# A sliding-window attention block on one core: weighted values started ahead of the second softmax, with a fixed order on a shared port

## The chip, the core and the metric

The kernel runs on one core of a Trainium2 chip. The engines are called by the names of the profile: PE (TensorE, matmuls), DVE (VectorE), ACT (ScalarE), POOL (GpSimd) and SP (the queue that issues most DMAs). In this program SBUF is the memory that the engines work from, and PSUM, of eight banks, the one that matmuls write to. The metric is device microseconds of one execution. Each of the kernels in the experiments ran beside the kernel before on the same chip.

## The reference, cut to what matters

```python
xn = layernorm(x)                       # x: 1 x 2048 x 640
q, k, v = split(xn @ wqkv)              # 32 heads of 20
# each position sees 8 positions: its own, 2 back, 4 back, ... 14 back
logits = einsum("bhsd,bhswd->bhsw", q, k[window]) * scale
attn = softmax(logits, axis=-1)
o = einsum("bhsw,bhswd->bhsd", attn, v[window])
A = o @ wo
B = ((xn @ w_gate) * (xn @ w_up)) @ w_down      # 640 -> 1536 -> 640
return x + A + B
```

The large matmuls (projections, gate and up, down) are TensorE's. The window part is elementwise: products of q with shifted k on VectorE, their head sums as small matmuls, softmax on VectorE and ScalarE, then attention times shifted v on VectorE, the sum of two window halves on GpSimd, and again a head sum as small matmuls.

## The kernel before

The kernel does not write its instructions in order. Small generators yield tasks with priorities and dependencies; a scheduler with a model of durations (`occ`, in us) picks the order for each engine once, when the program is built, and puts in the semaphore waits. On the chip each engine then runs its fixed list. In the program, `lock` marks the instructions that are to be kept apart: VectorE steps with both inputs in SBUF, and GpSimd's; the changed kernel calls what they share a port. These are the parts that the change and the argument touch:

```python
def calm():            # may GpSimd read SBUF now? not during a softmax
    return all(("sm", x) in done or count.get(("logits", x), 0) < 2 for x in range(2))

def tokens():          # every add waits for the end of the softmaxes already placed
    return [("tok", x) for x in range(2) if ("sm", x) in done]

# softmax step on VectorE, both inputs in SBUF, lock=True: not beside a GpSimd op in the model
op("dve", lambda e: e.tensor_tensor(o, a, b, f), r=[a, b], w=[o], name=name, occ=occ, lock=True)

BATCH = (1, 4, 9, 14, 19)               # units after which head sums are made
def unit(u):                            # 20 units: 4 row blocks x 5 chunks of channels
    ...
    def mul(x, r0, nr):                 # attention (in PSUM) times shifted values (in SBUF)
        op("dve", lambda e: e.tensor_tensor(p, vw, a, ALU.mult), ..., occ=0.09 + 1.1 * nr)
    def add(x):                         # sum of the two window halves
        op("pool", lambda e: e.tensor_tensor(o, p[:, :, 0, :], p[:, :, 1, :], ALU.add), ..., occ=2.36, lock=True)
    ...
def sums(us):                           # head sums: 4 matmuls with 128x32 weights for each unit
    ...
    yield Task("pe", go, ..., banks=len(us), slack=0.7)
```

The head sums use one quarter of TensorE's columns at a time, so each batch of them sits in another tiling mode than the large matmuls around it. Of the eight PSUM banks two hold the attention weights; a batch of five units wants five of the other six at once.

Of the kernel before, what the change touches and what calls it, by code (L numbers as in the profile page):

```python
# [49 lines left out]
class Sched:  # L50
# [5 lines left out]
    def __init__(self, nc):  # L56
# [7 lines left out]
        self.t_lock = 0.0  # L64
        self.t_data = 0.0
# [42 lines left out]
    def deps_of(self, eng, rk, wk):  # L108
# [6 lines left out]
        for k in wk:  # L115
            st = self.state.get(k)
            if st is None:
                continue
            o, rds = st
            if o is not None and not (eng == "pe" and o.eng == "pe"):  # L120
                deps[o.idx] = o
            for q in rds:
                if inorder and q.eng == eng and not q.dma and eng != "dve":
                    continue
                deps[q.idx] = q
        return deps

    def op(self, eng, fn, r=(), w=(), dma=False, name="", occ=None, lat=None, lock=False, nbytes=0, mode=0, group=None, extra=0.0, acc=0.0, land=None):
# [7 lines left out]
        deps = self.deps_of(eng, rk, wk)  # L136
        if occ is None and not dma:
            occ = 0.1
# [45 lines left out]
        if dma:  # L184
# [7 lines left out]
            else:  # L192
                g = self.groups[group]
                g[1].append(X)
                X.event = (g[0], 16)
        self.ops.append(X)
# [152 lines left out]
def build_kernel(nc, A_x, A_wqkv, A_wo, B_x, B_w_gate, B_w_up, B_w_down, out):  # L349
# [43 lines left out]
    sv_free = list(range(NS))  # L393
# [69 lines left out]
    def dma(o, i, r=(), w=(), name="", eng="sp", group=None, land=None):  # L463
# [10 lines left out]
       r=[IDENT[:]], w=[IDENT[:]], name="ident", occ=0.4)  # L474
    op("pool", lambda e: e.memset(G[:], 0.0), w=[G[:]], name="g0", occ=0.2)
# [58 lines left out]
    def front(t):  # L534
# [11 lines left out]

        def sqrt():
            op("act", lambda e: e.activation(sd, mv[:, 1:2], ACT.Sqrt, bias=EPSC[:, 0:1]), r=[("mv", t), EPSC[:]],  # L548
               w=[("sd", t)], name=f"sd{t}", occ=0.25)
            mark("sd", t)  # L550

        def recip():
            op("dve", lambda e: e.reciprocal(rstd, sd), r=[("sd", t)], w=[("rstd", t)], name=f"rstd{t}", occ=0.16)
            mark("rstd", t)
            if t >= N_DVE_A:
                op("dve", lambda e: e.tensor_scalar(nmr, mv[:, 0:1], rstd, -1.0, op0=ALU.mult, op1=ALU.mult),
                   r=[("mv", t), ("rstd", t)], w=[("nmr", t)], name=f"nmr{t}", occ=0.13)
# [27 lines left out]
        yield Task("act", sqrt, r=[("mv", t)], prio=p - 1)  # L585
        yield Task("dve", recip, r=[("sd", t)], prio=p)
# [192 lines left out]
    def calm():  # L779
        return all(("sm", x) in done or count.get(("logits", x), 0) < 2 for x in range(2))  # L780

    def tokens():
        return [("tok", x) for x in range(2) if ("sm", x) in done]
# [7 lines left out]
    def products():  # L791
        rows = {j: [] for j in range(NJ)}
        holds = {}
        for j, kind in ORDER:
# [4 lines left out]
            else:  # L799
                if len(QUAD.get(j, ())) == 2 and j not in holds:  # L800
# [4 lines left out]
            if len(rows[j]) == 10 - 3 * len(QUAD.get(j, ())):  # L805
                K.spawn(logits(j, rows[j]))

# [17 lines left out]
    def q_bank(j, c, hold):  # L825
# [7 lines left out]
        def copy():  # L833
            evac([(QT[:, j, c, :], PS[:, hold[0], :], JB)], f"qev{j}_{c}")
# [13 lines left out]
    def wide(j, slots, hold):  # L848
        halves = [(r, q0) for r in QUAD[j] for q0 in (0, 2)]
        acc, parts = {}, {1: [], 0: []}  # L850
        for c0 in (0, 2):
            for i, (r, q0) in enumerate(halves):
                f = []
                for c in (c0, c0 + 1):
                    yield lambda: len(hold[c]) > 0 and len(usable(j)) > 0
                    k = slot(j)
# [6 lines left out]
                    def go(o=o, qb=qb, kv=kv, q=q, rk=rk):  # L863
                        X = op("dve", lambda e: e.tensor_tensor(o[:], qb, kv, ALU.mult), r=[q, rk], w=[o[:]],  # L864
# [50 lines left out]
    def logits(j, slots):  # L915
# [7 lines left out]
        def go(*bs):  # L923
            for i, e in enumerate(slots):
                n, s, r = e[:3]
                b, i, nt = bs[1 - r], i - (0 if r else n1), n1 if r else len(slots) - n1
                for a in range(4):
                    o = PS[32 * a:32 * a + 32, b, :].rearrange("p (q s) -> p q s", q=4)
                    x = s[:, :, a * TS:(a + 1) * TS]
                    op("pe", (lambda o, x, i, a: lambda e: e.matmul(o, G[:], x, start=(i == 0), stop=(i == nt - 1),  # L930
                                                                   tile_position=(0, 32 * a)))(o, x, i, a),
# [25 lines left out]
    def softmax(x):  # L957
        def tt(o, a, b, f, name, occ):
            return Task("dve", lambda: op("dve", lambda e: e.tensor_tensor(o, a, b, f), r=[a, b], w=[o], name=name, occ=occ,
                                          lock=True), r=[a, b], w=[o], prio=10, lock=True)  # L960
# [8 lines left out]
        def sub():  # L969
            op("dve", lambda e: e.tensor_tensor(L[:], L[:], bc(M3[:], 8), ALU.subtract), r=[L[:], m3], w=[L[:]], name="lsub",  # L970
               occ=1.2, lock=True)

        def exp():
            op("act", lambda e: e.activation(L[:], L[:], ACT.Exp), r=[L[:]], w=[L[:]], name="exp", occ=1.9)

        def recip():
            op("act", lambda e: e.activation(s3, s3, ACT.Ln), r=[s3], w=[s3], name="rln", occ=0.4)
            op("act", lambda e: e.activation(R, s3, ACT.Exp, scale=-1.0), r=[s3], w=[R], name="rs", occ=0.4)
# [431 lines left out]
```

## Time and profile before

The time before is 268.65 us (median of runs, 268.47 to 268.7).

| | before |
|---|---|
| span of the profiled run | 266.8 us |
| PE busy | 261.3 us (98%) |
| DVE, POOL, ACT busy | 82%, 50%, 40% |
| POOL's adds: first starts, last ends | 131.05, 244.42 us |
| last head sums start | 244.42 us in the chain |

To read it: 98% on TensorE and a list of its waits in which no other engine stands after the first 10 us say that every microsecond of matmul is a microsecond of the kernel. The other engines matter only when they are late. By the starts in the trace, the last unit's four head sums begin at 245.22 us, 0.8 us after its last add ends, so there was next to no slack.

### The profile page before, as it was taken

How to read it: one execution, taken by the hardware profiler on the slowest of the kernel's cores; microseconds unless marked ns; L12 is line 12 of the kernel's file. 1: busy time of each engine (PE TensorE's matmuls, PEld its weight loads, DVE VectorE, ACT ScalarE, POOL GpSimd, SP SyncE). 2: the span in 40 equal slices, each digit the busy share in tenths (PEclk: the TensorE clock that was granted, in tenths of full speed). 3: DMA queues.
4: the chain of work that ended last, by engine and by line, in shares of the span. 5: the costliest groups of instructions: out<-in, count | busy, mean ns of one | idle time of the engine just before them, and what ended most of it. 6: DMA issues, size and time to landing. Idle time of an engine off the chain costs nothing.

```text
span 266.8 us, 4468 instructions
## 1 busy us (share of the span) xinstructions
PE 261.3 (98%) x1771; PEld 152.6 (57%) x1788; DVE 218.3 (82%) x278; ACT 107.6 (40%) x193; POOL 132.4 (50%) x83
## 2 busy tenths in 40 slices
PE   7999999999999999999999999999999999999996
PEld 5996965444444444444444446764577547754775
DVE  4678899999999996379999899988998999981221
ACT  3469998556732122255434442007500460016000
POOL 1000000000007359700399999977999799979000
PEclk9999999999999999999999999999999999999999
DMA  7974789502226997193426733656345633130101
GB/s 213 374 207 81 195 107 371 213 0 98 101 49 161 192 234 178 9 333 81 114 49 142 170 80 87 185 162 168 80 129 152 184 96 89 49 98 2 49 27 49
DMA packets 40933, 35.75 MB, mean 134 GB/s; under 512 B 16080, under 2 KB 39120, under 8 KB 40912
## 3 DMA queue, kind: packets, MB, share of 16 engines
q1 hardware_dynamic: 40096, 33.31, 46.0%
q0 software_dynamic: 576, 2.10, 4.1%
q8 instruction: 14, 0.23, 0.4%
q10 hardware_dynamic: 240, 0.05, 0.1%
q14 instruction: 7, 0.06, 0.1%
HBM read 25.07 MB, written 5.26 MB: 114 GB/s over the span
## 4 chain that ended last, share of the span: by engine, by line
PE 96%; DVE 1%; DMA 1%; issue 1%; ACT 0%
PE PS L1195 39%; PE PS L1277 28%; PE PS L655 22%; PE PS L930 3%; PE PS L687 2%; PE PS L1144 2%; DMA XST<-in_A_x_dram 1%; PE PS L599 0%; DVE STATS L542 0%; ACT XNT L611 0%; DVE XNS L563 0%; DVE XNT L609 0%; DVE FOUT L1290 0%; ACT SD L548 0%; DVE MV L545 0%
## 5 line engine op out<-in xcount | busy, mean ns | idle before, releaser
L1096 POOL TENSOR_TENSOR SV<-PV 128x1024 bf16<-128x1024 f32 x40 | 93.2, 2361 | 20.4 <-DVE LOG L981 19.4
L1091 DVE TENSOR_TENSOR PV<-VX,PS 128x1024 f32<-128x1024 bf16 (+1 forms) x56 | 91.9, 1669 | 2.5 <-POOL SV L1096 2.3
L655 PE MATMUL PS<-XNT,WQKV 128*128 128x512 bf16 (+2 forms) x384 | 60.2, 315 | 0.4 <-issue 0.2
L1195 PE MATMUL PS<-XNT,WG 128*128 128x512 bf16 x238 | 59.4, 379 | 0.2
L1195 PE MATMUL PS<-XNT,WU 128*128 128x512 bf16 x231 | 57.7, 379 | 0.4 <-issue 0.2
L655 PEld LDWEIGHTS PS<-XNT,WQKV 128*128 128x128 bf16 x390 | 37.9, 112 | 21.8 <-ACT LOG L941 0.8
L1195 PEld LDWEIGHTS PS<-XNT,WG 128*128 128x128 bf16 x240 | 23.3, 98 | 28.5 <-issue 0.8
L1195 PEld LDWEIGHTS PS<-XNT,WU 128*128 128x128 bf16 x240 | 23.4, 98 | 28.2 <-ACT LOG L941 0.4
L819 DVE TENSOR_TENSOR PRD<-QT,KT 128x2048 bf16<-128x2048 bf16 x32 | 36.8, 1215 | 0.0
L1290 DVE TENSOR_TENSOR FOUT<-PS,XR 128x320 bf16<-128x320 f32 (+1 forms) x33 | 15.7, 477 | 18.4 <-PE PS L1277 18.3
L1277 PE MATMUL PS<-WD,HT 128*128 128x320 bf16 x192 | 28.5, 299 | 0.0
L660 ACT ACTIVATE HT<-PS 128x512 bf16<-128x512 f32 x24 | 14.3, 596 | 31.6 <-PE PS L1195 31.6
L1277 PE MATMUL PS<-WO,OT 128*128 128x320 bf16 (+1 forms) x165 | 26.6, 295 | 0.0
L890 POOL TENSOR_TENSOR PRF<-PRF,PRF 128x1024 f32<-128x1024 f32 x4 | 9.4, 2348 | 31.2 <-DVE PRF L864 31.2
L660 ACT ACTIVATE UX<-PS 128x512 bf16<-128x512 f32 x14 | 8.4, 597 | 39.5 <-PE PS L1195 39.5
L949 POOL MEMSET LOG<- 32x6 bf16 (+6 forms) x7 | 0.4, 96 | 47.6 <-ACT LOG L941 47.6
L1204 DVE TENSOR_TENSOR HT<-HT,PS 128x512 bf16<-128x512 bf16 x23 | 15.7, 684 | 9.5 <-PE PS L1195 7.4
L1277 PEld LDWEIGHTS PS<-WD,HT 128*128 128x128 bf16 x192 | 18.6, 98 | 8.0 <-issue 0.4
L1277 PEld LDWEIGHTS PS<-WO,OT 128*128 128x128 bf16 x165 | 15.9, 98 | 5.9
L864 DVE TENSOR_TENSOR PRF<-PS,KT 128x1024 f32<-128x1024 f32 x16 | 19.0, 1216 | 0.3 <-DMA PRF<-PRF 0.3
L660 ACT ACTIVATE XNT<-PS 128x512 bf16<-128x512 f32 x12 | 7.2, 598 | 25.5 <-PE PS L1195 25.5
L542 DVE BATCH_NORM_STATS2 STATS<-XST 128x6 f32<-128x320 bf16 x32 | 14.6, 472 | 2.5 <-DMA XST<-in_A_x_dram 2.5
(62 smaller groups left out, 235.7 us busy)
## 6 DMA issues: line engine op xcount, KB each, us to landing
VX<-v_scratch SPq DMA_DIRECT2D x80, 130.0 KB, 2.9
XST<-in_A_x_dram SPq DMA_DIRECT2D x16, 160.0 KB, 5.7
v_scratch<-VST SPq DMA_DIRECT2D x4, 640.0 KB, 4.2
XR<-in_A_x_dram SPq DMA_DIRECT2D x16, 160.0 KB, 2.7
out_dram<-FOUT SPq DMA_DIRECT2D x15, 160.0 KB, 1.8
PRF<-PRF POOLq DMA_DIRECT2D x4, 512.0 KB, 8.7
WG<-in_B_w_gate_dram SPq DMA_DIRECT2D x1, 1920.0 KB, 8.6
WU<-in_B_w_up_dram SPq DMA_DIRECT2D x1, 1920.0 KB, 12.0
```

Of the source, the lines that this page charges most:

```text
L542: op("dve", lambda e: e.bn_stats(o, a), r=[a], w=[("st", t, i)], name=f"bn{t}_{i}", occ=0.49)
L655: op("pe", (lambda o, l, x, c, first: lambda e: e.matmul(o, l, x, start=first, stop=(c == NCH - 1)))(o, l, x, c, first), r=[l, x], w=[o], ...
L660: X = op("act", (lambda o, i: lambda e: e.activation(o, i, ACT.Copy))(o, i), r=[i], w=[o], name=name, occ=0.12 + n * 0.9e-3)
L819: op("dve", lambda e: e.tensor_tensor(s[:], qb, kv, ALU.mult), r=[q, rk], w=[s[:]], name=f"prod{j}_{r}_{c}", occ=1.15, lock=True)
L864: X = op("dve", lambda e: e.tensor_tensor(o[:], qb, kv, ALU.mult), r=[q, rk], w=[o[:]], name=f"prow{j}_{r}_{c}_{q0}", occ=1.17)
L890: yield Task("pool", lambda: op("pool", lambda e: e.tensor_tensor(x, x, y, ALU.add), r=[x, y] + tokens(), w=[x], name=name, occ=2.36, lock ...
L1091: op("dve", lambda e: e.tensor_tensor(p, vw, a, ALU.mult), r=[vv] + rk, w=[p], name=f"pv{u}_{x}_{r0}", occ=0.09 + 1.1 * nr)
L1096: X = op("pool", lambda e: e.tensor_tensor(o, p[:, :, 0, :], p[:, :, 1, :], ALU.add), r=[p[:]] + tokens(), w=[o], name=f"pva{u}_{x}", occ= ...
L1195: op("pe", (lambda l, x, c: lambda e: e.matmul(PS[:, b, :], l, x, start=(c == 0), stop=(c == NCH - 1)))(l, x, c), r=[l, x], w=[PS[:, b, :] ...
L1204: X = op("dve", lambda e: e.tensor_tensor(h, h, PS[:, hold[1], :], ALU.mult), r=[h, PS[:, hold[1], :]], w=[h], name=f"h{m}_{j}", occ=0.65)
L1277: op("pe", (lambda l, x, i: lambda e: e.matmul(dst, l, x, start=(i == 0), stop=(i == n - 1)))(l, x, i), r=[l, x], w=[PS[:, b, :]], name=f" ...
L1290: X = op("dve", lambda e: e.tensor_tensor(o, PS[:, b, 0:wid], xr, ALU.add), r=[PS[:, b, :], xr], w=[o], name=f"fin{t}_{nb}", occ=0.15 + wi ...
```

## The change

Its intent is to use GpSimd's 19.4 idle us ahead of and during the second softmax. The model's `calm` (no add during a softmax) becomes a rule that fits an add into a gap when it does not push the next softmax step by more than 0.3 us, and explicit waits make VectorE and GpSimd alternate on the chip in just that order. The first adds go to two output buffers that nobody else needs by then. With early adds, the first head sums can be one batch of five. Beside that, square roots and reciprocals of the layer norm are made for pairs of tiles.

```diff
+        if lock:
+            deps.update({d.idx: d for d in self.port["pool" if eng == "dve" else "dve"]})
...
-    sv_free = list(range(NS))
+    sv_free = [3, 4, 0, 1, 2]
...
-    def calm():
-        return all(("sm", x) in done or count.get(("logits", x), 0) < 2 for x in range(2))
+    def room(occ, ready=0.0):
+        def f():
+            if count.get(("logits", 0), 0) >= 2 and ("sm", 0) not in done:
+                return False
+            return due[0] == INF or max(K.t["pool"], K.t_lock, ready) + occ <= due[0] + SLIP
+        return f
+    calm = room(2.36)
     def tokens():
-        return [("tok", x) for x in range(2) if ("sm", x) in done]
+        return []
...
-    BATCH = (1, 4, 9, 14, 19)
+    BATCH = (4, 9, 14, 19)
     def vx_loads():
-        yield num(NJ, "lg")
+        yield have("products")
...
+    GROUPS = ((4, 5), (6, 7), (8, 9), (10, 11), (12, 13), (14, 15))
```

(Cut: the selection matrix made by GpSimd at the start, some ordering of ScalarE's reads, the time of the residual's loads, the place of the first two attention copies, and the rule that lets multiplications of gate and up go to GpSimd earlier.)

More of the change, by code (lines that the diff above doesn't have):

```diff
@@ L64, in __init__ @@
         self.t_lock = 0.0
+        self.port = {"dve": [], "pool": []}
         self.t_data = 0.0
@@ L122, in deps_of @@
             for q in rds:
-                if inorder and q.eng == eng and not q.dma and eng != "dve":
+                if inorder and q.eng == eng and not q.dma and eng != "dve" and not (eng == "act" and k[0] == "ps"):
                     continue
@@ L195, in op @@
                 X.event = (g[0], 16)
+        if lock:
+            self.port[eng] = [X] if eng == "dve" else self.port[eng] + [X]
+            if eng == "dve":
+                self.port["pool"] = []
         self.ops.append(X)
@@ L474, in build_kernel @@
        r=[IDENT[:]], w=[IDENT[:]], name="ident", occ=0.4)
+    op("pool", lambda e: e.memset(SEL[:], 0.0), w=[SEL[:]], name="sel", occ=0.1)
+    for q in range(4):
+        op("pool", (lambda q: lambda e: e.affine_select(SEL[:], SEL[:], pattern=[[-1, 32]], compare_op=ALU.not_equal, fill=1.0,
+                                                        base=-32 * q, channel_multiplier=1))(q),
+           r=[SEL[:]], w=[SEL[:]], name=f"sel{q}", occ=0.2)
     op("pool", lambda e: e.memset(G[:], 0.0), w=[G[:]], name="g0", occ=0.2)
@@ L545, in aggr @@
             op("dve", lambda e: e.bn_aggr(mv, st), r=[("st", t, 0), ("st", t, 1)], w=[("mv", t)], name=f"bnag{t}", occ=0.2)
+        ts = next((g for g in GROUPS if t in g), (t,))
+        t0, t1 = ts[0], ts[-1] + 1
         def sqrt():
-            op("act", lambda e: e.activation(sd, mv[:, 1:2], ACT.Sqrt, bias=EPSC[:, 0:1]), r=[("mv", t), EPSC[:]],
-               w=[("sd", t)], name=f"sd{t}", occ=0.25)
-            mark("sd", t)
+            o, i = SD[:, t0:t1, 0:1], MV[:, t0:t1, 1:2]
+            op("act", lambda e: e.activation(o, i, ACT.Sqrt, bias=EPSC[:, 0:1]), r=[("mv", k) for k in ts] + [EPSC[:]],
+               w=[("sd", k) for k in ts], name=f"sd{t}", occ=0.25)
+            for k in ts:
+                mark("sd", k)
         def recip():
-            op("dve", lambda e: e.reciprocal(rstd, sd), r=[("sd", t)], w=[("rstd", t)], name=f"rstd{t}", occ=0.16)
-            mark("rstd", t)
+            o, i = SD[:, t0:t1, 1:2], SD[:, t0:t1, 0:1]
+            op("dve", lambda e: e.reciprocal(o, i), r=[("sd", k) for k in ts], w=[("rstd", k) for k in ts], name=f"rstd{t}", occ=0.16)
             if t >= N_DVE_A:
-                op("dve", lambda e: e.tensor_scalar(nmr, mv[:, 0:1], rstd, -1.0, op0=ALU.mult, op1=ALU.mult),
-                   r=[("mv", t), ("rstd", t)], w=[("nmr", t)], name=f"nmr{t}", occ=0.13)
+                n, m = SD[:, t0:t1, 2:3], MV[:, t0:t1, 0:1]
+                op("dve", lambda e: e.scalar_tensor_tensor(n, m, -1.0, o, op0=ALU.mult, op1=ALU.mult),
+                   r=[x for k in ts for x in (("mv", k), ("rstd", k))], w=[("nmr", k) for k in ts], name=f"nmr{t}", occ=0.13)
+            for k in ts:
+                mark("rstd", k)
         def apply():
@@ L584, in front @@
         yield Task("dve", aggr, r=[("st", t, 1)], prio=p)
-        yield Task("act", sqrt, r=[("mv", t)], prio=p - 1)
-        yield Task("dve", recip, r=[("sd", t)], prio=p)
+        mark("mv", t)
+        if t == ts[-1]:
+            yield Task("act", sqrt, r=[("mv", t)], prio=p - 1)
+            yield Task("dve", recip, r=[("sd", t)], prio=p)
+        yield have("rstd", t)
         if t >= NXN:
@@ L777, in slot @@
         return n
-    def calm():
-        return all(("sm", x) in done or count.get(("logits", x), 0) < 2 for x in range(2))
+    INF = 1e9
+    due = [INF]
+    def room(occ, ready=0.0):
[5 more added lines that the diff above has]
+    calm = room(2.36)
     def tokens():
-        return [("tok", x) for x in range(2) if ("sm", x) in done]
+        return []
     def k_view(j, r, c, q0, nq):
@@ L793, in products @@
         holds = {}
-        for j, kind in ORDER:
+        for at, (j, kind) in enumerate(ORDER):
             if kind == "w":
@@ L799, in products @@
             else:
-                if len(QUAD.get(j, ())) == 2 and j not in holds:
+                if len(QUAD.get(j, ())) == 2 and j not in holds and (j, "w") == ORDER[at + 1]:
                     yield from fetch(j, 0, holds.setdefault(j, {c: [] for c in range(4)}))
@@ L806, in products @@
                 K.spawn(logits(j, rows[j]))
+        mark("products")
     def narrow(j, r, c, slots):
@@ L833, in copy @@
         def copy():
-            evac([(QT[:, j, c, :], PS[:, hold[0], :], JB)], f"qev{j}_{c}")
+            o, i = QT[:, j, c, :], PS[:, hold[0], :]
+            op("act", lambda e: e.activation(o, i, ACT.Copy), r=[i], w=[o, ("qev", j, c)], name=f"qev{j}_{c}", occ=0.58)
             for _ in range(4):
@@ L855, in wide @@
                     yield lambda: len(hold[c]) > 0 and len(usable(j)) > 0
+                    yield num(4, "qk", 0, j, c)
                     k = slot(j)
@@ L863, in go @@
                     def go(o=o, qb=qb, kv=kv, q=q, rk=rk):
-                        X = op("dve", lambda e: e.tensor_tensor(o[:], qb, kv, ALU.mult), r=[q, rk], w=[o[:]],
+                        X = op("dve", lambda e: e.tensor_tensor(o[:], qb, kv, ALU.mult), r=[q, rk, ("qev", j, c)], w=[o[:]],
                                name=f"prow{j}_{r}_{c}_{q0}", occ=1.17)
@@ L929, in go @@
                     x = s[:, :, a * TS:(a + 1) * TS]
-                    op("pe", (lambda o, x, i, a: lambda e: e.matmul(o, G[:], x, start=(i == 0), stop=(i == nt - 1),
-                                                                   tile_position=(0, 32 * a)))(o, x, i, a),
+                    op("pe", (lambda o, x, i, a, nt: lambda e: e.matmul(o, G[:], x, start=(i == 0), stop=(i == nt - 1),
+                                                                   tile_position=(0, 32 * a)))(o, x, i, a, nt),
                        r=[G[:], x], w=[o], name=f"lg{j}_{r}_{i}_{a}", occ=0.054, lat=0.4, mode=1)
@@ L958, in tt, with go @@
         def tt(o, a, b, f, name, occ):
-            return Task("dve", lambda: op("dve", lambda e: e.tensor_tensor(o, a, b, f), r=[a, b], w=[o], name=name, occ=occ,
-                                          lock=True), r=[a, b], w=[o], prio=10, lock=True)
+            def go():
+                X = op("dve", lambda e: e.tensor_tensor(o, a, b, f), r=[a, b], w=[o], name=name, occ=occ, lock=True)
+                due[0] = INF if name == "ssum3" else X.end
+            return Task("dve", go, r=[a, b], w=[o], prio=10, lock=True)
         L = LOG[x]
@@ L971, in sub @@
                occ=1.2, lock=True)
+            due[0] = INF
         def exp():
-            op("act", lambda e: e.activation(L[:], L[:], ACT.Exp), r=[L[:]], w=[L[:]], name="exp", occ=1.9)
+            X = op("act", lambda e: e.activation(L[:], L[:], ACT.Exp), r=[L[:]], w=[L[:]], name="exp", occ=1.9)
+            due[0] = X.end
         def recip():
             op("act", lambda e: e.activation(s3, s3, ACT.Ln), r=[s3], w=[s3], name="rln", occ=0.4)
-            op("act", lambda e: e.activation(R, s3, ACT.Exp, scale=-1.0), r=[s3], w=[R], name="rs", occ=0.4)
+            X = op("act", lambda e: e.activation(R, s3, ACT.Exp, scale=-1.0), r=[s3], w=[R], name="rs", occ=0.4)
+            due[0] = X.end
         def attn():
-            op("dve", lambda e: e.tensor_tensor(L[:], L[:], bc(RS[:], 8), ALU.mult), r=[L[:], R], w=[L[:], ("tok", x)], name="attn",
+            op("dve", lambda e: e.tensor_tensor(L[:], L[:], bc(RS[:], 8), ALU.mult), r=[L[:], R], w=[L[:]], name="attn",
                occ=1.2, lock=True)
+            due[0] = INF
         def move():
@@ L992, in softmax @@
         yield num(2, "logits", x)
+        if x:
+            due[0] = max([0.0] + [d.end for d in K.deps_of("dve", K.keys(L[:]), ()).values()])
         if x:
@@ L1040, in weighted @@
         yield have("atx", 0)
+        yield have("products")
         def take(a, b):
@@ L1045, in weighted, with at_copy @@
         yield Task("act", take, banks=2, prio=0, contig=True)
+        for r in range(2):
+            yield Task("act", lambda: at_copy(0, r), r=[ATX[0][:, 0, r, :]], w=[PS[:, at_bank[r], :]], prio=1)
         for u in range(NU):
             yield from unit(u)
+    def at_copy(j, r):
+        o, i = PS[:, at_bank[r], :], ATX[j // 2][:, j % 2, r, :]
+        op("act", lambda e: e.activation(o, i, ACT.Copy), r=[i], w=[o], name=f"atp{j}_{r}", occ=0.55)
     def unit(u):
@@ L1056, in unit @@
             sv_free.extend(range(NS, len(SV)))
-        yield lambda: len(sv_free) > 0
+        yield lambda: len(sv_free) > 0 and (sv_free[0] in (3, 4) or count.get(("lg",), 0) >= NJ)
         sv_of[u] = sv_free.pop(0)
@@ L1072, in unit @@
         v = VX[:, u % NVX]
-        def at_copy(r):
-            o, i = PS[:, at_bank[r], :], ATX[j // 2][:, j % 2, r, :]
-            op("act", lambda e: e.activation(o, i, ACT.Copy), r=[i], w=[o], name=f"atp{j}_{r}", occ=0.55)
         def mul(x, r0, nr):
@@ L1108, in adder @@
             yield Task("pool", lambda: add(x), r=[slots[x][:]], w=[sv[:, 2 * x:2 * x + 2, :]], prio=10, lock=True)
-        if c in (0, NCH - 1):
+        if c == NCH - 1 or (c == 0 and j):
             for r in range(2):
                 if c == 0:
-                    yield Task("act", lambda: at_copy(r), r=[ATX[j // 2][:, j % 2, r, :]],
+                    yield Task("act", lambda: at_copy(j, r), r=[ATX[j // 2][:, j % 2, r, :]],
                                w=[PS[:, at_bank[r], :]], prio=1)
@@ L1163, in on_pool @@
     def on_pool(j, m):
-        return ("sm", 1) in done and m < 11 and ucount[0] - count.get(("hp",), 0) < HP_MAX
+        return count.get(("lg",), 0) >= NJ and m < 11 and ucount[0] - count.get(("hp",), 0) < HP_MAX
     def gu(j):
@@ L1220, in pmul @@
                     def pmul():
-                        op("pool", lambda e: e.tensor_tensor(h, h, us, ALU.mult), r=[h, us], w=[h], name=f"hp{m}_{j}",
+                        op("pool", lambda e: e.tensor_tensor(h, h, us, ALU.mult), r=[h, us] + tokens(), w=[h], name=f"hp{m}_{j}",
                            occ=1.15, lock=True)
@@ L1227, in after @@
                     yield num(k0, "hp")
-                    yield calm
+                    yield room(1.15)
                     yield Task("pool", pmul, r=[h, us], w=[h], prio=HP_PRIO, lock=True)
@@ L1238, in xr_loads @@
     def xr_loads():
-        yield have("xnt", NT - 1)
+        yield num(NJ, "lg")
         yield have("vx", NVX)
@@ L1311, in dn_piece @@
         K.spawn(tail())
+    SLIP = 0.3
     N_PE_T = 4
     BN_AFTER = (4,)
+    GROUPS = ((4, 5), (6, 7), (8, 9), (10, 11), (12, 13), (14, 15))
     N_DVE_A = 6
@@ L1341, in misc @@
         yield have("xnt", NT - 1)
-        def sel():
-            for q in range(4):
-                a, b = SEL[32 * q:32 * q + 32, :], IDENT[32 * q:32 * q + 32, 32 * q:32 * q + 32]
-                op("dve", (lambda a, b: lambda e: e.tensor_copy(a, b))(a, b), r=[b], w=[a], name=f"sel{q}", occ=0.1)
         def preload(e):
@@ L1351, in misc @@
         free.append(NPR - 1)
-        yield Task("dve", sel, prio=19)
         yield Task("act", lambda: op("act", preload, name="exp_preload", occ=1.3), prio=6)
```

## The prediction

> **What bounds the kernel now.** I read four views of the kernel before, in this order: the page, the waits of TensorE, the chain that ended last in order of time, and the windows of the stretch that the change is about.
>
> From the page, the busy line and the chain by engine:
>
> ```profile
> PE 261.3 (98%) x1771; PEld 152.6 (57%) x1788; DVE 218.3 (82%) x278; ACT 107.6 (40%) x193; POOL 132.4 (50%) x83
> ...
> PE 96%; DVE 1%; DMA 1%; issue 1%; ACT 0%
> ```
>
> TensorE (PE) is busy in 98% of a span of 266.8 us, and 96% of the chain that ended last is matmuls. A busy PE is not by itself a PE at its limit, so I looked at what it waits for and at its pace. Its waits, whole:
>
> ```profile
> PE PS L639 <- DVE ZERO L469: 1.3, 1, 1.3
> PE PS L687 <- DVE XNT L609: 0.3, 1, 0.3
> PE PS L655 <- issue: 0.2, 1, 0.2
> PE PS L1195 <- issue: 0.2, 1, 0.2
> ```
>
> The 1.3 us are the wait before the warm-up matmuls, and the 0.3 us lie at 8 us, in the first tiles. After that TensorE waits for no other engine, in 250 us. The chain in order of time (start, length, what) shows the pace and the end:
>
> ```profile
> 178.97 0.05 issue
> 179.02 9.66 PE PS L1195 x44
> 188.68 1.19 PE PS L1144 x20
> ...
> 236.91 7.50 PE PS L1195 x34
> 244.42 1.19 PE PS L1144 x20
> 245.61 18.64 PE PS L1277 x153
> 264.25 0.02 issue
> 264.27 0.33 DVE FOUT L1290
> ```
>
> L1195 is the gate and up projection, L1144 the head sums, L1277 the down projection. 44 matmuls of 512 columns took 9.66 us, 0.2195 us each, and that average is too high by the records that are missing; the timeline has a full five starting every 1.08 us, 0.216 us for each matmul. At 136 in 18.58 us the 320-column ones take 0.1366 us. Ratio of time to columns is 0.00042 us in both, so they run at one rate per column, the page gives the granted clock as 9 tenths or more in every slice, and the windows give 1.00. TensorE is **at its own rate and without a gap** from about 8 us to 264.25 us. After it come one add of 0.33 us and the store.
>
> Last, the stretch that the change fills, from the end of GpSimd's last sum of products (107.00 + 4.64 = 111.64) to its first add of weighted values (131.05), and the rest up to the last head sums (244.42). The columns are busy us of PE, weight load, VectorE, ScalarE, GpSimd:
>
> ```profile
> 111.64:131.05 19.41, 19.30 (x100) 8.56 (x102) 15.64 (x21) 9.95 (x17) 0.01 (x1) 1.00 0.59 160
> 131.05:244.42 113.37, 113.01 (x717) 65.08 (x724) 102.20 (x87) 33.65 (x60) 106.31 (x53) 1.00 0.45 117
> ```
>
> GpSimd does nothing for 19.41 us, then is busy 106.31 of 113.37 us (94%). The page says why it was idle:
>
> ```profile
> L1096 POOL TENSOR_TENSOR SV<-PV 128x1024 bf16<-128x1024 f32 x40 | 93.2, 2361 | 20.4 <-DVE LOG L981 19.4
> ```
>
> All 40 adds wait for the last step of softmax 2 on VectorE. But in both windows TensorE is busy all but 0.1 and 0.4 us. GpSimd is the densest helper, and just in time: its last add starts at 242.1 and takes 2.36, so it ends near 244.4, where the head sums start. It holds nobody up.
>
> **What the Trainium skill says.** "SBUF — State Buffer", section "Who interferes with whom", states that a VectorE instruction with two SBUF inputs contends with a GpSimd instruction that reads SBUF, that the pair is an exclusive lock, and that one with at most one SBUF input does not contend. The trace agrees with the last part: VectorE's products L1091 read one input from PSUM and run beside GpSimd's 40 adds, which all take 2345 to 2392 ns. The first part this trace can't show, because the program keeps softmax 2 and the adds apart. "Perfetto Trace Analysis", section "Tensor Engine Instruction (MATMUL, LD_WEIGHTS)", states that matmul ends are estimated; that is why I judged the pace from starts. "TensorEngine Tiling (Array Packing)", section "Key Properties", states that a change of tiling mode drains TensorE. The head sums (128x32 weights) are such a change, and the trace gives its cost below.
>
> **The change part by part.**
>
> 1. Weighted values ahead of softmax 2. The value loads wait for the last products instead of all logits; at the front the adds use two buffers (the third and fourth) that no logit input occupies; adds and the locked steps of softmax 2 alternate by explicit waits, so that an add goes in only where it fits with 0.3 us of slip. From 111.64 to the first step of softmax 2 at 118.68 there are 7.0 us, enough for two or three adds of 2.36. Softmax 2's own locked steps on VectorE are 0.69 + 0.75 + 1.22 + 1.23 + 0.68 + 0.42 + 1.22 = 6.2 us of the 12.3 us to 130.97; the other 6 us hold two adds, beside the exponential (1.91) and the reciprocal (0.42 + 0.42). So four to five of the 40 adds move ahead, 9 to 12 us of GpSimd's chain, and its last add should end near 233 to 236 in place of 244.4. On the path that sets the end: **0.0 us**, since TensorE does not wait for it in the kernel before.
>
> 2. Four batches of head sums in place of five: (0 to 4), (5 to 9), and so on, in place of (0, 1), (2 to 4), and then as now. The 80 matmuls stay. In the chain the batches take 0.61 us (8 matmuls), 0.76 (12) and 1.19 (20). The first two become one of 20: 0.61 + 0.76 - 1.19 = **0.18 us less**, with the drain of one batch. It is on TensorE, which is the bound, so it counts in full. I take 0.2.
>
> 3. Front: ScalarE's square root and VectorE's reciprocal of tiles 4 to 15 in pairs. Six instructions of 0.28 us fewer on ScalarE, six reciprocals of 0.16 and five scalings of 0.21 fewer on VectorE: 1.7 us and 2.0 us. The first of each pair waits for the second, one rate of about 1.6 us per tile. The projections want both of tiles 4 and 5 together anyway, and between tile 5's transpose (issued after 18.3 + 0.45, landing 2.9 us later, near 21.7) and its use (the copies of tile 4 and 5's projections begin at 26.9) stand some 4 us of values' projections. On the path: 0.
>
> 4. The selection matrix is made by GpSimd at the start in place of four VectorE copies later. GpSimd is idle there (it ends at 2.4 us), the matrix is first used after 140 us: 0. A wait of ScalarE on its own reads of PSUM, and of the wide products on a key: ordering only, ScalarE is 40% busy: 0.
>
> 5. Lifting of the gate for the multiplications on GpSimd (14 of 1.16 us) to the end of the logits instead of softmax 2: again off the path: 0.
>
> Sum: 268.65 - 0.2 = 268.45, and I say **268.4 us**.
>
> **The rivals.** (a) The gain is large: if softmax 2's wait (19.4 us) delayed the end, the time would fall by some of the 9 to 12 us, to about 257 to 260. For it speaks the largest idle time of GpSimd; against it, the whole list of TensorE's waits and the two windows, in which there is no gap to close. Nearly excluded.
>
> (b) The new waits stall TensorE. A step of softmax 2 that now waits for an add of 2.36 us holds up VectorE, in order, and behind it the multiplications (0.69 us) that free the PSUM banks of gate and up. One pair of gate and up takes 2.16 us, and after two banks for the weights six are left, three pairs, so a VectorE late by about 4 us does not reach TensorE. In the kernel before products of 2.29 us already stand ahead of these multiplications from 131 us on, and no wait showed. And five banks at once for the first batch of head sums can leave TensorE a hole, if the batch is put amid gate and up. I give this 0.3 to 1.5 us, with a chance of about a fifth, and a stall of over 5 us 2 to 3%.
>
> (c) GpSimd's buffers fill: with five buffers and a first batch of five, adds must wait until that batch is summed, which returns part of the 9 to 12 us. It would cost nothing at the end, for the reason of part 1.
>
> **Range and chances.** Below, a wall: TensorE's work is unchanged but for one drain, so even all known gaps (0.3 + 0.2 + 0.2 us) give no less than about 267.8. Above, rival (b). Range **267.8 to 269.4**. Two per cent are 5.4 us: faster by that would need TensorE work that nothing removes (0.01), slower a new stall in a schedule that was laid out by a model of these durations (0.03), so within 2%: 0.96.
>
> **What would show it.** GpSimd's first add before 118 us and its last ending by 236; its idle time before L1096 down by 9 to 12 us from 20.4, with new waits of GpSimd on VectorE and back, of 2 us at most. Four groups of 20 head sums in the chain. TensorE's waits still short of 1 us beyond the warm-up, and busy 98%. It would be wrong if a wait of TensorE on VectorE or ScalarE appeared between 112 and 165 us, or if in the first 30 us the paired square roots made it wait for a transpose.

## The result

The changed kernel took 268.49 us (268.1 to 268.62, 4 runs) against 268.65 us. The ratio is 0.9993, with a 95% interval of 0.9976 to 1.001; a second set of 5 runs gave 268.31 us and 0.9996 (0.9984 to 1.0009). So it is the same time. (A ratio is the mean time of one kernel's runs over that of the other's of the same rounds, so not quite the ratio of the medians that are quoted.)

Under the unchanged time, GpSimd's part has moved. Busy times, POOL's adds, and the chain by engine and line on the page of the changed kernel (line numbers are those of the changed file: L1144 is the add, L1139 the weighted values, L1192 the head sums):

```profile
PE 261.1 (98%) x1771; PEld 152.8 (57%) x1788; DVE 210.5 (79%) x254; ACT 110.0 (41%) x194; POOL 141.5 (53%) x95
...
PE 90%; ACT 6%; issue 1%; DMA 1%; DVE 1%
...
L1144 POOL TENSOR_TENSOR SV<-PV 128x1024 bf16<-128x1024 f32 x40 | 93.4, 2358 | 12.3 <-DVE PV L1139 5.0
```

Idle time ahead of the adds fell from 20.4 to 12.3 us, by 8.1 and not by the 9 to 12 that the prediction named. GpSimd also does 21 multiplications of gate and up in place of 14, 17 of them ahead of its last add in place of 13: about 4.6 us more work there. The 6% of ACT in the chain are no loss: in a second profile of the same kernel, below, the chain shows 0% of it. GpSimd's timeline of the changed kernel (start, length, what, and in brackets the idle time before it) shows where the adds went:

```profile
108.09 7.13 POOL L1144 TENSOR_TENSOR SV<-PV 128x1024 bf16<-128x1024 f32 x3
118.31 2.36 POOL L1144 TENSOR_TENSOR SV<-PV 128x1024 bf16<-128x1024 f32 x1 [3.09 <-DVE LOG L1009]
120.63 1.16 POOL L1269 TENSOR_TENSOR HT<-HT,UX 128x512 bf16<-128x512 bf16 x1
124.31 4.67 POOL L1144 TENSOR_TENSOR SV<-PV 128x1024 bf16<-128x1024 f32 x2 [2.52 <-DVE SM L996]
...
231.26 4.65 POOL L1144 TENSOR_TENSOR SV<-PV 128x1024 bf16<-128x1024 f32 x2
```

Six adds are done before the last step of softmax 2 (L1023, which ends at 131.7 us), and the last add ends at 235.91 us, 8.5 us earlier than before. The brackets are the new order at work: GpSimd waits for a softmax step, 3.09 and 2.52 us. The chain by engine and TensorE's waits, whole (total, times, longest), in the second profile of the changed kernel:

```profile
PE 97%; DMA 1%; DVE 1%; ACT 0%; issue 0%
...
PE PS L662 <- DVE ZERO L476: 1.3, 1, 1.3
PE PS L710 <- DVE XNT L632: 0.3, 1, 0.3
PE PS L622 <- DVE XNS L583: 0.2, 1, 0.2
```

All three waits lie in the first 10 us. The end of its chain in order of time (L1243 is gate and up, L1325 the down projection):

```profile
228.33 8.63 PE PS L1243 x40
236.96 1.19 PE PS L1192 x20
238.16 7.66 PE PS L1243 x35
245.82 18.53 PE PS L1325 x153
```

The last head sums now stand 7.66 us of gate and up ahead of the down projection, where before they stood right at its door. The end did not move. I took this second profile because it has every matmul's record; some are missing from the first, and each missing one looks like a gap of up to 0.22 us.

### The profile page after: what moved, and what is told of

It reads as the page before. It is cut to its first block, busy times and chain, and to the rows that moved or that the text cites. A ratio compares the mean times of both kernels' runs of the same rounds, so it can differ in the third digit from the quotient of the medians.

```text
span 266.9 us, 4455 instructions
## 1 busy us (share of the span) xinstructions
PE 261.1 (98%) x1771; PEld 152.8 (57%) x1788; DVE 210.5 (79%) x254; ACT 110.0 (41%) x194; POOL 141.5 (53%) x95
## 4 chain that ended last, share of the span: by engine, by line
PE 90%; ACT 6%; issue 1%; DMA 1%; DVE 1%
PE PS L1243 38%; PE PS L1325 28%; PE PS L678 17%; PE PS L966 3%; ACT XNS L589 3%; PE PS L710 2%; PE PS L1192 2%; DMA XST<-in_A_x_dram 1%; ACT QT L683 1%; ACT VST L683 1%; ACT KT L683 1%; PE PS L622 0%; ACT SD L564 0%; DVE STATS L554 0%; ACT HX L683 0%
## 5 line engine op out<-in xcount | busy, mean ns | idle before, releaser
L1144 POOL TENSOR_TENSOR SV<-PV 128x1024 bf16<-128x1024 f32 x40 | 93.4, 2358 | 12.3 <-DVE PV L1139 5.0
L1139 DVE TENSOR_TENSOR PV<-VX,PS 128x1024 f32<-128x1024 bf16 (+1 forms) x54 | 91.6, 1727 | 5.1 <-POOL SV L1144 3.2
L1243 PE MATMUL PS<-XNT,WG 128*128 128x512 bf16 x237 | 59.0, 379 | 0.3
L1243 PE MATMUL PS<-XNT,WU 128*128 128x512 bf16 x232 | 57.9, 379 | 0.4 <-issue 0.2
L1243 PEld LDWEIGHTS PS<-XNT,WU 128*128 128x128 bf16 x240 | 23.4, 98 | 28.4 <-ACT OT L1201 0.4
L1243 PEld LDWEIGHTS PS<-XNT,WG 128*128 128x128 bf16 x240 | 23.4, 98 | 28.2 <-issue 0.4
L1325 PE MATMUL PS<-WD,HT 128*128 128x320 bf16 x192 | 28.4, 300 | 0.0
L1325 PE MATMUL PS<-WO,OT 128*128 128x320 bf16 (+1 forms) x165 | 26.7, 295 | 0.0
L1325 PEld LDWEIGHTS PS<-WD,HT 128*128 128x128 bf16 x192 | 18.6, 98 | 8.0 <-DVE HX L1252 0.4
L683 ACT ACTIVATE UX<-PS 128x512 bf16<-128x512 f32 x21 | 12.6, 600 | 25.0 <-PE PS L1243 24.6
L1325 PEld LDWEIGHTS PS<-WO,OT 128*128 128x128 bf16 x165 | 15.9, 98 | 5.9
L683 ACT ACTIVATE HX<-PS 128x512 bf16<-128x512 f32 x12 | 7.2, 597 | 26.4 <-PE PS L1243 26.4
L1252 DVE TENSOR_TENSOR HT<-HT,PS 128x512 bf16<-128x512 bf16 x20 | 13.6, 682 | 3.8 <-PE PS L1243 3.4
```

Of the source, the lines that this page charges most:

```text
L683: X = op("act", (lambda o, i: lambda e: e.activation(o, i, ACT.Copy))(o, i), r=[i], w=[o], name=name, occ=0.12 + n * 0.9e-3)
L1139: op("dve", lambda e: e.tensor_tensor(p, vw, a, ALU.mult), r=[vv] + rk, w=[p], name=f"pv{u}_{x}_{r0}", occ=0.09 + 1.1 * nr)
L1144: X = op("pool", lambda e: e.tensor_tensor(o, p[:, :, 0, :], p[:, :, 1, :], ALU.add), r=[p[:]] + tokens(), w=[o], name=f"pva{u}_{x}", occ= ...
L1243: op("pe", (lambda l, x, c: lambda e: e.matmul(PS[:, b, :], l, x, start=(c == 0), stop=(c == NCH - 1)))(l, x, c), r=[l, x], w=[PS[:, b, :] ...
L1252: X = op("dve", lambda e: e.tensor_tensor(h, h, PS[:, hold[1], :], ALU.mult), r=[h, PS[:, hold[1], :]], w=[h], name=f"h{m}_{j}", occ=0.65)
L1325: op("pe", (lambda l, x, i: lambda e: e.matmul(dst, l, x, start=(i == 0), stop=(i == n - 1)))(l, x, i), r=[l, x], w=[PS[:, b, :]], name=f" ...
```

## The experiments

The mean granted clock is 1.00 in all profiles except three, which say so below by their windows: there it fell with long waits of TensorE.

The theory: TensorE is the bound; of the change only the one batch of head sums less is on it, about 0.2 us; the early adds give slack and no time. Rivals: the early adds give time; the new waits cost time that the batch gives back; the saving is hidden.

### The changed kernel again

No edit.

> The changed kernel once more, for a narrower interval. Theory (TensorE is the bound, and the change takes one drain of about 0.2 us from it): 268.2 to 268.5 us, ratio 0.9985 to 1.000. Rival (the early start of the adds gives something at the end): below 267.5 us. From the first 128-column projection to the last matmul the trace should again show about 0.2 to 0.3 us less than the kernel before, whatever the first load took.

Measured: 268.31 us, ratio 0.9996 (0.9984 to 1.0009). TensorE took 244.987 us from the first 512-column matmul to the last matmul. This stretch, read from starts in the trace, leaves out the first 19 us, whose length varies by up to 0.6 us between profiles. It is the fine scale for the next ones. The first profiles of the two kernels each lack the first record of this stretch; with it put back where its weight load stands, they give 245.207 us before and 244.988 us after. So the whole change saves TensorE 0.22 us.

### Five batches again

```diff
-    BATCH = (4, 9, 14, 19)
+    BATCH = (1, 4, 9, 14, 19)
```

> The changed kernel with the head sums in five batches again (2, 3, 5, 5, 5). Theory: one more drain on TensorE, 0.1 to 0.2 us longer than the changed kernel, 268.5 to 268.8 us, and the stretch of TensorE from the first projection to the last matmul longer by 0.18 us. Rival (the drain is hidden): no difference in that stretch.

Measured: 268.58 us, ratio 1.0005 (0.9992 to 1.0017); the stretch is 245.209 us, 0.222 us more. Both profiles have all 1788 matmuls, and the starts show the two parts of it: the last full matmul before a batch is followed after 0.309 us in place of 0.216, and the batches of 8 and 12 take 0.548 and 0.765 us where one of 20 takes 1.195, 0.118 us more. In the clock of whole executions 0.2 us stays inside the noise of a run.

What costs TensorE 0.2 us gives GpSimd much more. The last two adds with five batches, and then with four:

```profile
225.03 4.65 POOL L1144 TENSOR_TENSOR SV<-PV 128x1024 bf16<-128x1024 f32 x2
```

```profile
231.23 4.65 POOL L1144 TENSOR_TENSOR SV<-PV 128x1024 bf16<-128x1024 f32 x2
```

With five batches the adds end at 229.7 us, 6.2 us earlier than with four (235.9). So the larger first batch takes back 6.2 us of the slack that other parts of the change make. The prediction's rival (c) said this: with five output buffers, adds must wait until the first batch of five is summed.

### Four batches alone, in the kernel before

```diff
-    BATCH = (1, 4, 9, 14, 19)
+    BATCH = (4, 9, 14, 19)
...
-    DN_KEEP = 3
+    DN_KEEP = 5
```

> The kernel before with four batches alone (2 and 3 made one of 5; the down projection may hold no half-done banks, since five of the six are wanted at once). Theory: if TensorE still finds work, 0.2 us less than before, 268.4 us. Rival: without the early adds the batch of five and the strict banks make TensorE wait for GpSimd at its last batch, 0.5 to 3 us more than before; then four batches need the early start.

Measured: 270.56 us, ratio 1.008 (1.0068 to 1.0093), 2.2 us slower: the rival. The second line was forced. Without it the scheduler found no order at all: pieces of the down projection held PSUM banks while they waited for the head sums, and the head sums waited for five banks. The control with that line alone follows below. The end of the chain of this kernel (L1096 is the add, L1144 the head sums):

```profile
244.54 2.32 POOL SV L1096
246.86 2.32 POOLq L339
249.18 0.04 issue
249.22 0.39 PE PS L1144 x2
```

The adds end at 249.2 us, later than in the kernel before (244.4), and TensorE waits 1.6 us for the last one. The trace fits full output buffers: the first ten adds fill all five, the first batch runs from 159.6 to 160.8 us, and the eleventh add comes after it, with idle time ahead of it. In the kernel before it starts at 158.8 us with none.

```profile
164.41 2.35 POOL L1096 TENSOR_TENSOR SV<-PV 128x1024 bf16<-128x1024 f32 x1 [3.98 <-DVE PV L1091]
```

So the saved drain needs slack on GpSimd from somewhere. That it must be the early adds is not shown: the run after next does without them, and its four batches cost nothing.

### The control for the rule on banks

```diff
-    DN_KEEP = 3
+    DN_KEEP = 5
```

> The kernel before with only the rule for banks that three of the earlier experiments needed (no half-done banks of the down projection held while head sums are outstanding). It is their control. Theory: the rule is nearly free, at most 0.5 us, since before the head sums are done as gate and up end; then the 2.2 us of the kernel before with four batches belong to the batch, and 7.5 us of the one with doubled adds to the adds. Rival: the rule alone costs about 2 us, and those two readings shrink by it.

Measured: 268.58 us, ratio 0.9992 (0.9976 to 1.0009). The rule costs nothing by itself that whole executions show (its stretch, 245.324 us, is 0.12 us longer than the kernel before's), so the 2.2 us above are the batch's, and the comparisons below stand.

### The early adds undone

```diff
         def adder(x, slots=slots, sv=sv, add=add):
+            yield have("sm", 1)
             yield calm
```

> The changed kernel with one part undone: the adds on GpSimd wait until softmax 2 is done, as before. Theory: GpSimd's last add ends near 242 to 246 us in place of 235.9, and the time stays within 0.5 us of 268.5, because TensorE doesn't wait for it. Rival (the early start is worth time): 2 to 8 us longer.

Measured: 268.22 us, ratio 0.9992 (0.9978 to 1.0006), and TensorE's stretch 244.987 us, the same to the nanosecond. The first add starts at 123.9 and the last ends at 240.5 us. So the early start is worth no time here, as expected; but the last add came 4.6 us later, not the 6 to 10 that I had written. Softmax 2 itself ends at 123.8 us here, 7.2 us earlier than in the kernel before, so this run still holds what other parts of the change moved.

### The layer norm tile by tile again

```diff
-    GROUPS = ((4, 5), (6, 7), (8, 9), (10, 11), (12, 13), (14, 15))
+    GROUPS = ()
```

> The changed kernel with square roots and reciprocals of the layer norm tile by tile, as before. Theory: VectorE's products end 1 to 3 us later, GpSimd's first add begins 1 to 3 us later than 108.1 us, and the time stays within 0.4 us of 268.5. Rival (pairing shortened TensorE's first 35 us): 0.3 us or more longer, and seen before 40 us.

Measured: 268.32 us, ratio 0.9998 (0.998 to 1.0016); the stretch 244.989 us. VectorE's products end at 103.5 us in place of 99.7 and 100.4 in the two profiles of the changed kernel, the first add starts at 111.6 in place of 108.1, and the last ends at 240.1 in place of 235.9. So the pairs, undone alone, are worth 4.2 us of the slack, and the early adds 4.6. That the two sum to 8.8, near the 8.5 measured, is chance: four batches take back 6.2 us, and each run has its order laid out anew, so the parts don't simply add. Parts 4 and 5 of the prediction were not undone alone.

### Is the slack real: GpSimd's work made longer

Four of the 40 adds are done twice, in both kernels, with the rule on banks of the control.

```diff
-            X = op("pool", ..., name=f"pva{u}_{x}", occ=2.36, lock=True)
+            for _ in range(2 if x == 0 and 10 <= u < 14 else 1):
+                X = op("pool", ..., name=f"pva{u}_{x}", occ=2.36, lock=True)
```

> The kernel before with four of GpSimd's 40 adds done twice (same result), 4 x 2.36 = 9.4 us more on GpSimd, and no half-done banks held by the down projection. Theory (before, the adds end just in time): the last add ends near 254 us, TensorE waits for it, and the time grows by 6 to 9 us, 275 to 278 us. Rival (GpSimd has slack before as well): 268.7 us.

> The changed kernel with the same four adds done twice and the same rule for banks. Theory (the early start made about 8.5 us of slack): the last add ends near 245 us, TensorE does gate and up until 245.8 us, and the time stays at 268.3 to 269.5 us. Rival (the slack is not usable): 272 us or more.

Measured: the kernel before 276.24 us, ratio 1.0282 (1.0267 to 1.0297), 7.5 us slower; the changed kernel 268.33 us, ratio 0.9989 (0.9972 to 1.0005), not slower at all, with its last add ending at 244.5 us. The 9.4 us of extra adds cost the one 7.5 us and the other nothing. (In both, the scheduler also took multiplications off GpSimd: it does 10 in place of 14, and 19 in place of 21. In the kernel before the last add so ends at 252.1 us and not at the 254 expected.) The 7.5 us are not all waiting. TensorE's wait for GpSimd in the lengthened kernel before:

```profile
PE PS L1145 <- POOL SV L1097: 4.6, 2, 2.7
```

And two windows after it (columns as in the prediction; the first number after the counts is the granted clock):

```profile
252.20:256.00 3.80, 3.80 (x15) 1.97 (x16) 0.49 (x1) 0.60 (x1) 0.00 (x0) 0.50 0.00 0
256.00:260.00 4.00, 4.00 (x23) 2.50 (x22) 0.49 (x1) 0.00 (x0) 0.00 (x0) 0.72 0.01 2
```

It waited 4.6 us, in two pieces of 2.7 and 1.9 with two matmuls between. After it the clock was 0.50 for 3.8 us and 0.72 for 4.0: 3.8 x 0.50 + 4.0 x 0.28 = 3.0 us of matmul time lost. 4.6 + 3.0 = 7.6, the 7.5 us. My expectation had the size right by luck, as its make-up was wrong; it had only waiting.

### What the slack is worth when TensorE is faster

The fifth chunk of gate and up is left out for three of four row blocks, 72 matmuls, in both kernels, with the rule on banks. The result is wrong, though the comparison with the reference let it pass: that path adds little to the sum.

```diff
+                n = NCH - 1 if j else NCH
-                for c in range(NCH):
+                for c in range(n):
```

> The kernel before with 72 matmuls of gate and up left out (the fifth chunk for three of four row blocks; wrong result on purpose), 72 x 0.2158 = 15.5 us less TensorE work. Theory: TensorE is no longer the bound, GpSimd's chain to about 244 us is, and the time falls by 2 to 5 us only, to 263 to 267 us. Rival (TensorE alone is the bound and nothing stands behind it): 253 us.

> The changed kernel with the same 72 matmuls left out (wrong result on purpose). Theory: GpSimd's chain ends some 8.5 us earlier than before, so the time is 255 to 259 us, about 8 us under the kernel before with the same cut. Rival (the early start is worth nothing even then): the same time as the kernel before with the cut.

Measured: the kernel before 268.89 us, ratio 1.0014 (0.9999 to 1.003); the changed kernel 259.91 us, ratio 0.968 (0.9656 to 0.9703). The kernel before gains nothing at all from 15.5 us less matmul work, less than I expected: its adds end at 245.8 us, and TensorE waits 9.1 us for them and runs at a lower clock after the waits (0.61 for 4.0 us after the last one). The changed kernel with the cut is 8.8 us under the kernel before; it too is just outside what I expected, with 3.4 us of waits and a clock of 0.65 for 4.2 us behind them. In both I had left out what a wait does to the clock. Between the two kernels with the cut the change is worth 9.0 us. TensorE's waits for GpSimd in the two, before first:

```profile
PE PS L1144 <- POOL SV L1096: 9.1, 5, 3.4
```

```profile
PE PS L1192 <- POOL SV L1144: 3.4, 2, 1.9
```

### The fixed order taken away

```diff
-        if lock:
-            deps.update({d.idx: d for d in self.port["pool" if eng == "dve" else "dve"]})
```

The order on VectorE, ScalarE and GpSimd is that of the changed kernel, instruction for instruction, in the two traces; only the waits between VectorE and GpSimd that no data needs are gone.

> The changed kernel without the fixed order on the shared port: adds of GpSimd and the locked steps of VectorE's softmax 2 run whenever their data is there. Theory: the two engines meet, some steps of softmax 2 or some adds take visibly longer than 0.69/1.22 us and 2.36 us in the trace (one held for the other), but TensorE hides it and the time stays within 0.5 us of 268.5. Rival (the order is what keeps TensorE fed): over 270 us.

Measured: 271.94 us, ratio 1.0128 (1.0113 to 1.0143), 3.4 us slower than the kernel before. My theory fell here: I had expected TensorE to hide it. VectorE's timeline without the fixed order, the steps of softmax 2 with GpSimd's adds meeting them (L994 the maxima and sums, L1021 the last step; L1142 the add):

```profile
116.44 3.62 DVE L994 TENSOR_TENSOR M<-M 128x512 bf16<-128x512 bf16 x2
...
124.63 3.00 DVE L994 TENSOR_TENSOR SM<-LOG 128x1024 f32<-128x1024 bf16 x1
...
134.91 3.02 DVE L1021 TENSOR_TENSOR LOG<-LOG,RS 128x2048 bf16<-128x2048 bf16 x1
```

```profile
115.89 2.73 POOL L1142 TENSOR_TENSOR SV<-PV 128x1024 bf16<-128x1024 f32 x1 [0.44 <-DVE PV L1137]
...
124.19 2.35 POOL L1142 TENSOR_TENSOR SV<-PV 128x1024 bf16<-128x1024 f32 x1 [4.28 <-DVE PV L1137]
...
134.51 2.34 POOL L1142 TENSOR_TENSOR SV<-PV 128x1024 bf16<-128x1024 f32 x1
```

The same steps in the changed kernel:

```profile
116.22 0.75 DVE L996 TENSOR_TENSOR M<-M 128x512 bf16<-128x512 bf16 x2
...
121.82 1.22 DVE L996 TENSOR_TENSOR SM<-LOG 128x1024 f32<-128x1024 bf16 x1
...
130.46 1.22 DVE L1023 TENSOR_TENSOR LOG<-LOG,RS 128x2048 bf16<-128x2048 bf16 x1
```

Take the second pair: the add runs from 124.19 to 126.54; the sum that VectorE began at 124.63 ends at 127.63, which is 126.54 plus 1.09, so nearly its whole 1.22 us came after the add's end. In all three pairs a step is held until the add is done, and does not share with it (in the first pair the second of the two steps is then held by GpSimd's multiplication as well). The three are 2.87, 1.78 and 1.80 us late, 6.4 us in all. VectorE runs its list in the same order in both traces, so what stands behind them is late as well: the multiplications that free PSUM banks, and the weighted values that GpSimd's adds read. TensorE's waits after the first 10 us:

```profile
PE PS L1241 <- DVE HT L1250: 1.4, 2, 1.2
...
PE PS L1190 <- POOL SV L1142: 0.9, 1, 0.9
...
PE PS L1241 <- ACT HT L681: 0.2, 1, 0.2
```

TensorE's stretch is 248.505 us, 3.5 us more than with the order. The granted clock stayed at 1.00 in this run, so these are waits alone. The list names 2.5 of the 3.5 us; it counts from the ends of matmuls, which are modelled. The starts give 3.1: twice 0.33 us (at 130.2 and 131.7 us) and once 1.40 (at 140.8) ahead of gate and up, and 1.05 in the first batch of head sums, for the last add that it needs. Next to the changed kernel VectorE is 2.7 us late after the first held step, when TensorE does not wait, 4.2 after the second and 6.0 after the third.

### The slack spent

Half of the logit sums of the third row block move from TensorE (12 small matmuls) to VectorE and GpSimd.

```diff
-    QUAD = {3: (1, 0)}
+    QUAD = {3: (1, 0), 2: (1,)}
...
-    HP_MAX = 2
-    ORDER = ((0, "n"), (1, "n"), (2, "n"), (3, "n"), (3, "w"))
+    HP_MAX = 3
+    ORDER = ((0, "n"), (1, "n"), (2, "w"), (2, "n"), (3, "n"), (3, "w"))
...
-    DN_KEEP = 3
+    DN_KEEP = 5
```

(Also `m < 11` became `m < 10` for the multiplications that may go to GpSimd.)

> The changed kernel with its new slack spent: for the third row block half of the logit sums move from TensorE (12 matmuls of 0.054 us less, 0.65 us) to VectorE and GpSimd, with up to three multiplications at a time on GpSimd. Theory: VectorE's products grow by 4 x 1.22 = 4.9 us and GpSimd has four more sums, 9.4 us; if the chain of adds ends by 245 us, the time is 267.7 to 268.0 us; if it ends later, TensorE waits by as much, 268.5 to 270 us. I expect the second, as 9.4 is more than the 8.5 us won.

Measured: 269.18 us, ratio 1.0017 (1.0002 to 1.0032), in the second range that was named. The last add ends at 246.05 us, and the stretch is 245.685 us: 0.70 us more than the changed kernel with 0.65 us less matmul work. The slack was overspent, but not by waits for the adds, as I had written. Of TensorE's waits after the first 10 us the list has only this:

```profile
PE PS L1325 <- ACT OT L1201: 0.5, 3, 0.2
```

The starts give it as four gaps between 246.6 and 248.5 us, 1.32 us together: after the last head sums TensorE goes straight on to the output projection, whose inputs ScalarE is still copying. That is the 0.70 and the 0.65. Which of the edits left TensorE no other work there, no run shows. This one version beats neither kernel beyond noise.

## Why the prediction was right or wrong

**The time and the bound: right.** 268.4 us was said, 268.49 and 268.31 us came. TensorE has no wait after the first tiles in the changed kernel either, and undoing the early adds or the pairs leaves its stretch at 244.987 and 244.989 us. That is the shown cause of the missing gain.

**Part 2, one drain less, 0.18, taken as 0.2 us: right**, and 0.222 us in the comparison of five batches with four. That the sum came so near is partly luck. The prediction's difference of the chain's pieces missed the slower step into a batch (0.309 - 0.216 = 0.09 us), and its 0.61 us for the first batch is 0.55 by the starts, as a missing record lengthened it. What four batches do to GpSimd, 6.2 us less slack in the changed kernel and 2.2 us more time in the kernel before, stands in the prediction only as rival (c), and there as free of cost at the end; it took the parts as independent.

**Part 1, early adds: no time, right; size, off.** The last add was to end at 233 to 236 us and ended at 235.91, but for another sum. Four or five adds ahead of the end of softmax 2 became six, and the 9 to 12 us given to the early start measure 4.6 when it is undone alone. Two pieces were missing from it. One is **part 3**: on the path the pairs are worth 0 as said, but they end the products 3.1 to 3.8 us earlier, and undone alone they cost 4.2 us of slack. The prediction had 2.0 us of saved VectorE instructions there and took them as worth nothing further on; how 2.0 became 3.1 or more I did not trace. The other is the larger first batch, which takes back 6.2 us. That the end of the sum fell into the range is luck.

**Rival (a)**, a large gain, is out. **Rival (b)** named the wrong side of the waits: the chance of a fifth for a stall was put on the new waits, which stall nothing; the stall comes, 3.4 us of it, when they are taken out. The prediction had a step's length under the order only and took the alternation as a cost, up to a wait of 2 us (they were up to 3.1 us, on GpSimd, which has the time). Its estimate that VectorE may be about 4 us late before TensorE feels it fits that run: no wait at 2.7 us, two short ones at 4.2, and the long one at 6.0.

**Rival (c)**, full buffers, came true: four batches end the adds 6.2 us later than five in the changed kernel, and 4.4 us later in the kernel before with the rule for banks (249.2 against 244.8). "It would cost nothing at the end" held in the changed kernel, and not in the kernel before.

On the skill's pages: the page "SBUF — State Buffer", section "Who interferes with whom", says that a VectorE instruction with two SBUF inputs and a GpSimd instruction that reads SBUF block each other; the run without the order now shows it (3.00 in place of 1.22 us). The page "TensorE: Matmul & The Clock Gate", section "What's actually happening", states that the array falls to half clock after an idle window of about 3.4 us; the lengthened kernel before shows 0.50 after two waits of 2.7 and 1.9 us that were 0.4 us apart, so there the clock fell though the idle time was broken.

## What to carry to other kernels

When one engine is busy without a gap, a change that moves another engine's work forward changes slack and not time; measure that slack by lengthening the work until the time moves, for it decides what the next change is worth. Two engines that meet on a port need their order fixed where their chain feeds the bound: the explicit wait that looks like a cost may be what keeps it off the path, as the 3.4 us here show. And judge parts of a change by undoing each one in the changed kernel as well as by adding it to the old one: here one part alone is slower, while undoing it costs nearly nothing. Look then at every run's slack, and do not take a sum of parts that comes out near the whole for an account of it.

## What the Trainium skill lacked or had wrong

- "TensorE: Matmul & The Clock Gate", section "What's actually happening", gives one idle window of about 3.4 us for the fall to half clock. Here waits of 2.7 and 1.9 us with two matmuls between them were enough (0.50 for 3.8 us, then 0.72 for 4.0), while one wait of about 1.6 us (four batches in the kernel before) left it at 1.00. How busy a stretch may be for the clock still to fall, the page does not say.
- "TensorEngine Tiling (Array Packing)", section "Key Properties", says that a change of mode drains the engine and gives no figure. Here one more batch of 128x32 matmuls between full ones cost 0.222 us: 0.09 in the step into it and 0.118 in it and behind it.
- "SBUF — State Buffer", section "Who interferes with whom": agreed with; the held step took 3.00 us in place of 1.22.
- "Perfetto Trace Analysis": the page has no word that matmul records can be missing. In two profiles here 17 of 1788 were, each a seeming gap of up to 0.22 us, as large as the effect looked for.
